# Transposing q and k of two batches by crossbar transfers in place of TensorE, in a fused attention and MLP kernel

## The chip, the cores and the metric

One core of one Trainium2 chip. The metric is device time in microseconds (us) of one execution; a median over several executions is quoted. Executions of one kernel differ by a per cent or two here. Each one carries a state, fast or slow (slow: more than 1.5% above the fastest of the same kernel). Ratios compare fast ones only; the medians in the tables are over all executions.

## The reference, cut to what matters

Four batches, eight heads, 768 rows, head size 64. Causal attention; three heads see every earlier key, five see the first 4 keys and a window of 64. The heads side by side form x of 768 x 512, which goes through a wave MLP:

```python
scores = q @ k.T / 8;  a = softmax(masked scores);  x = a @ v      # per batch and head
theta = x @ w_theta                                                # 512 x 512
zr, zi = x * cos(theta), x * sin(theta)
y = einsum('ts,bsd->btd', w_tok_r, zr) + einsum('ts,bsd->btd', w_tok_i, zi)   # the token mix, 768 x 768
u = x + y
out = u + maximum(u @ w_ch, 0)                                     # the channel matmul
```

The matmuls work on bf16. The inputs are so small (0.1 times normal draws) that the softmax is nearly uniform: an output wrong in q or k can still pass the comparison with the reference.

## The kernel before: the parts that matter

The program first writes down all steps with an engine, a duration and their dependencies. A list scheduler, steered by a long list of priorities (`TILT`), then fixes one order for each engine, and the steps are emitted in it. Each engine and each queue works through its own list in that order.

```python
def turn_qk(what, b, n):                 # 12 narrow transposes on TensorE into one PSUM bank: L395 in the profile
    pt = state["pt", what, n] = mine_bf()
    for j in range(NB):
        for x, h in enumerate(PAIRS[n]):
            nc.tensor.transpose(pt[64 * x:64 * x + 64, j * 128:(j + 1) * 128], state[what, b][:, h, j * D:(j + 1) * D], ident)

def keep_qk(what, n):                    # PSUM -> qT or kT, on VectorE or ScalarE
    dst = (qT if what == "q" else kT)[n]
    copy(dst.rearrange("d (p j) -> d p j", j=NB), state.pop(("pt", what, n))[:, :S].rearrange(...))

def load_v(b, half):                     # on the Sync queue, four heads at a time
    heads = slice(4 * half, 4 * half + 4)
    nc.sync.dma_start(out=v_room[:, heads]..., in_=v[b, heads]...)
# ...
# send_x and send_u: transposing transfers of x and u (128x512) from Sync; theta and channel matmuls wait for them
# load_qk: loads of q and k with a cast, issued from GpSimd; store: output from Sync
# mlp_steps: mix (3 groups), u, transpose of u, channel matmul, final operation, store
```

The softmax here doesn't subtract the row's maximum and nothing guards it: scores larger than these inputs give would overflow.

Of the kernel before, what the change touches and what calls it, by code (L numbers as in the profile page):

```python
# [25 lines left out]
    71383, 33577, 73294, -468, 272, 1817, 2121, 1841, 1484, 998, -351, -458, -9998906, -4244, 10993, 53854, -3405,  # L26
    6928, 42937, -27592, 3470, 440, -1170, -8668, 30584, 1187, 131611, 11003, 41350974, 22079, 7061, 59467, 66431,
    42364, 66838, 49232, 30363, 39667, 30343, 71323, 34095, 32360, 33997, 32661, 1599, -643, 481689, -687, 479643,
    10008299, 117742521, 135319420, 117742203, 135320132, 117742437, 135319441, 33665, 30756, 33818, 32757, 33944,
    32167, 96740665, 96740841, 96741207, 96740837, 96740995, -40086, 2489, -29404, 1496, 21511, 2417553, 21872,  # L30
    2417414, 1232, 23224485, 19914, 2417541, 36373805, 2417413, 41478, 20144064, 41910, 7510594, -1006, 10008162,
    27019, 10008687, 2317, -822, 71, 885, 30746, 4782, 28260, -700, 0, 851, 30200, 1234, 16671, -417, 8, -563,
    150, -315, 119, -744, 0, -2086, 0, 548, 3112, 184, 1256, -1791, 0, 218, 752, 196, 3175, -1205, 0, 71357, 6153,
    0, 32543, 49107, 31384, 1227, 34083, 31606, 41910, 2709, 478753, 42322, 1021, 20513511, 10009579, 33487,
    32376, 10009719, 3061386, 20516550, 22990, 135320173, 30384, 2419544, 52082, 68040, 33791, 31401, 59232,
    65497, 71091, 33781, 31241, 33656, 31212, 42036, 19480, 2416926, 79160287, 135318358, 36388668, 9882286,
    36359654, 9867371, 36386091, 9881900, 36360748, 9867822, 36380489, 9885853, 36359579, 16622892, 36360622,
    16626254, 36361168, 16622969, 36361066, 16623202, 4404, 16351, 59586, 28353, 4287, 16466, 36361251, 53261,
    16623326, 16375, 27903, 27573, 27919, 27740, 4295, 4300, 16459, 2029, 29794, 30117, 29643, 30164, 4475, -856,
    24, -2541, 30238, 13762, 8711, 13664, 36359955, 9868033, 53378, 28516, 4917, 16623645, 4811, 16623892, 7, 810,  # L40
    -2223, 740, 30630, 137, 686, 2190, 658, 5916, 2615, 6222, 0, 8869, 3362, -1287, 0, -358, -620, -1072, 378,
    -1088, 358, -1482, 0, -908, 3108, 3053, 2556, 3175, 1994, -541, 4029, -2027, 443, 3087, 6247, 7224, 7707,
    3524, 1446, 145, 28321, -1758, 3046, 3213, 1938, -265, 9029, 2043, 3371, 1753, 3145, 1901, 3091, 5532, 2593,
    3883, -1311, 3122, 3196, 1921, -469, 3313, 2509, -288, 569, 2781, 3713, 9243, 7431, 1470, 0, -192, 3831, 2019,
    0, 952, 2262, 2765, 1417, 4943, 2862, 3017, 627, 4671, 2631, 1041, 6646, 4670, 830, 1866, 27, 4080, 5248,
    5671, 6705, 5103, 5667, 5732, 5378, 7798, 3719, 5937, 5989, 4277, 5669, 5648, 5767, 10067, 15, 5805, 6197,
    3753, 6052, 4214, 4158, 27275, 4065, 3679, 484, 76, 699, 0, 8188, 2442, -2323, 3242, -771, 336, 0, 417, 3878,
    502, 6390, 0, 6397, 0, -201, -390, 2653, -1, 2536, 1439, 0, 27303, 4094, -1220, 699, 571, -377, 0, -2008,
    -550, 489, 1174, 4261, -521, 0, 2334, 3007, 3186, 357, 0, 539, 0, 381, 1594, 769, 681, -1176, 2403, 0, 1644,
    1424, 4167, 4774, -640, 3694, 4115, 1590, 52, 0, 10207, 10302, 17, 5487, 2487, 3322, 3685, 1958, -115, 0,  # L50
    1278, 435, 48, 4630, -7, 1570, 41, 4926, 2732, 2867, 316, -65, 3820, 5940, 46, 5714, -87, 4029, 6008, -900, 0,
    207, 3181, -1890, 0, 372, 425, 2534, 0, 2651, 0, 2938, 7089, 5815, 3035, 4150, -1419, 3038, 4396, -900, 4748,
    3928, 2180, -198, 4640, 4240, -232, 6156, 6885, 5623, 13470, 2411, 1320, 13077, 2453, 2898, 7265, 2931, 3846,
    2887, 7384, 303, 4693, 4266, 2983, 2820, 7808, 332, 2714, 7985, 7738, 3942, 2085, 7081, 13673, 1381, 1001, 97,
    13671, 1776, 2404, 0, 5385, 1277, 2572, 1913, 5381, 904, 2631, 0, 8668, 2704, -145, 1307, 12055, 2019, 142,
    1807, 2720, 2655, 1600, 11967, 4387, 5544, 4391, 5600, 4716, 3728, 2582, 1586, 1908, 1795, 1896, 2095, 3728,
    4504, 11880, 11792, 7607, 1480, 6181, -150, 2513, 3028, 3771, -520, 0, -904, 0, 1201, -1294, 774, 512, 5429,
    1558, 0, 4756, 4685, 3735, -27, 0, 1552, 0, 1212, 347, 0, 2223, 7107, 183, 0, -58, 525, 2032, 6140, 0, -349,
    0, 4456, 229, 3887, 3367, 1689, -826, 0, 13058, 12693, 2337, -246, 1411, -277, 787, 626, -2065, 0, 160, 1199,
    10944, 0, 566, 672, 136, 3705, 10380, 15055, 8015, -17, -1058, 0, 3989, 2971, 1172, 7388, -1070, 0, -401,  # L60
    1423, -2036, 0, 69, 7506, -199, -504, 1956, 8487, 284, 1558, -1901, 622, 1946, 496, 4131, -680, 1961, 7942,
    283, 1343, -1901, 2642, 0, 2935, 2901, -904, 0, 1807, 1884, 661, 0, 1498, 0, 8019, -368, -1831, 6187, 1508,
    13580, 7853, 1348, 13206, 5432, 3571, 1546, 14303, 6167, 1616, 13539, 8035, -553, 887, 6033, 3284, 1481, 8104,
    -515, 7983, -35, 5380, 3520, 4327, 2710, 14882, 4300, -225, 17476, 8037, -229, -2170, 8078, -355, -251, 5364,
    3027, 17524, 37247, 1593, 30869, 0, 37555, 1626, 31594, 0, 22131, 16141, 30282, 0, 21805, 16036, 30305, 41,
    4508, 977, 226, 1349, 2832, 1057, 18, 51, 2854, 2844, 89, 586, 8778, 8244, 8472, 4657, 2899, 2748, -123, -320,
    2283, 2087, 2174, 2098, 1672, 830, -790, -660, 5071, 4133, 3088, 3855, 7423, 7062, 9000, -975, -2753, 3331,
    5493, 1307, 31137, 0, 7964, 7870, 5312, 965, 29975, 54853, 5490, 15749, -619, 0, 587, 9022, 6186, 31738,
    30293, 285, 3736, 15797, -632, 0, 4912, 1715, -342, 1335, -509, 1610, 2359, -3159, -23, 0, 5374, 4362, 4287,
    16854, -304, 53, 2629, 2970, 285, 0, 4350, -993, 1817, 5218, -757, 1251, 2672, -1073, 1792, 0, 2872, 2629,  # L70
    2714, -1232, 767, 0, -1425, 1125, 2390, 0, 4905, 2655, -1663, -651, 2319, 3164, 28456, 141, 20332, 0, 2632,
    2284, -2379, 1034, 2273, 4363, 27747, 1034, 21235, 0, -669, 764, 12072, -454, 19612, 25792, 28797, 881, 21566,
    2456, 28301, 29807, 31171, 921, 30773, 934, 1327, 2527, 20772, 571, 28258, 1526, 1729, 1013, 679, -1128, 2221,
    2979, 21483, 744,
# [3 lines left out]
class Step:  # L78
# [7 lines left out]
    def __init__(self, on, fn, after, take, give, mode, bias, port, share):  # L86
        self.on, self.fn, self.after = on, fn, [a for a in after if a is not None]
        self.take, self.give, self.mode, self.bias, self.port, self.share = take, list(give), mode, bias, port, share
        self.eng = next(iter(on)) if len(on) == 1 else None
        self.users = 0  # L90
        self.slot = self.start = self.end = self.ns = None


class Plan:
# [18 lines left out]
    def add(self, on, ns, fn, after=(), take=None, give=(), mode=None, bias=0, port=False, share=None):  # L113
        s = Step(on if isinstance(on, dict) else {on: ns}, fn, after, take, give, mode, bias, port, share)
        for g in s.give:
            g.users += 1
        self.steps.append(s)
        return s

    def order(self, free):  # L120
# [8 lines left out]
        for s in reversed(self.steps):  # L129
            far = max(self.LATENCY[e][0] for e in s.on)  # L130
            near = min(self.LATENCY[e][1] for e in s.on)
            rank[s.n] = min(s.on.values()) + max((rank[n.n] + (near if len(s.on) == 1 and n.on.keys() == s.on.keys() else far) for n in later[s.n]), default=0)
# [24 lines left out]
        while events:  # L157
# [10 lines left out]
            for e in engines:  # L168
# [34 lines left out]
                if s.share:  # L203
                    o = "DMA" if e == "DMAH" else "DMAH"
                    rest = max(0, free.get(o, 0) - t) + sum(n.on[o] for n in ready.get(o, ()) if ready_at[n.n].get(o, 0) <= t)
                    ns += min(rest, ns * s.share) * (1 - 1 / s.share)
# [5 lines left out]
                far, near = self.LATENCY[e]  # L212
                heapq.heappush(events, (s.end, count, None))
# [19 lines left out]
def kernel(  # L233
# [40 lines left out]
    half_pi = const.tile([128, 1], F32, name="half_pi")  # L274

# [42 lines left out]
    def mine_bf():  # L318
        return mine().bitcast(BF16)
# [41 lines left out]

    def load_v(b, half):
# [627 lines left out]
```

## Time and profile before

| | before |
|---|---|
| median, three executions | 191.59 us (189.45 to 192.15) |
| span of the profiled execution | 188.3 us |
| TensorE / VectorE / ScalarE / GpSimd busy | 180.1 / 130.7 / 103.9 / 60.0 us |
| TensorE transposes of q and k (L395) | 384 matmuls, 8.0 + 7.7 us |
| queue of the Sync engine (q1) | 43256 packets, 17.65 MB, 43.5% |
| last mixing matmul to the end of the span | 181.72 to 188.3, 6.6 us |

The percentage of a queue is the time that its packets took, as a share of sixteen engines over the whole span. In a short stretch this share can exceed 1, so it is not a busy time; read it as pressure. A bank is a piece of PSUM, TensorE's output memory, and a pair is two of them; u, x, qT, vx and so on are the program's names for its tiles. PE in the profile is TensorE, DVE is VectorE, ACT is ScalarE, POOL is GpSimd, SP or SPq is the Sync engine's queue.

### The profile page before, as it was taken

Reading aid. Unit: us, or ns where it says so; the run is one execution under the profiler, and the core shown is the slowest. Engines: PE = TensorE matmul, PEld = TensorE weight load, DVE = VectorE, ACT = ScalarE, POOL = GpSimd, SP = SyncE. Lnnn points to the kernel's source line nnn. Section 1 sums busy time; section 2 is a strip of 40 time slices with the busy share of each in tenths; the row PEclk is TensorE's granted clock in tenths of the full one; section 3 lists DMA queues with packets and bytes.
Section 4 is the critical chain, followed back from the end, with each engine's and each line's share of the span. In section 5 each row is a group of like instructions: output and inputs, shape, how many; then the busy total and the mean of one; then the engine's idle time right before and its main releaser. Section 6 shows DMA issues by size and latency. Waiting matters only on the chain.

```text
span 188.3 us, 5126 instructions
## 1 busy us (share of the span) xinstructions
PE 180.1 (96%) x2143; PEld 101.2 (54%) x2143; DVE 130.7 (69%) x250; ACT 103.9 (55%) x129; POOL 60.0 (32%) x131
## 2 busy tenths in 40 slices
PE   6699989999999999999999999999999999999982
PEld 6546687764545874454447366444346564444430
DVE  7757696999855986997446466997249259935451
ACT  4488856698777707575780449686860356400010
POOL 7889878109737200005570020500320100000000
PEclk9999999999999999999999999999999999999999
DMA  5999999999999995978999952242344523234323
GB/s 175 173 188 205 200 206 204 208 207 222 147 234 274 196 136 139 209 158 187 181 128 228 104 159 41 61 95 111 87 111 58 168 59 79 61 120 106 108 111 113
DMA packets 56174, 28.06 MB, mean 149 GB/s; under 512 B 40408, under 2 KB 53080, under 8 KB 56152
## 3 DMA queue, kind: packets, MB, share of 16 engines
q1 hardware_dynamic: 43256, 17.65, 43.5%
q0 software_dynamic: 12896, 10.09, 36.1%
q8 instruction: 16, 0.26, 0.6%
q14 instruction: 6, 0.05, 0.1%
HBM read 25.71 MB, written 6.29 MB: 170 GB/s over the span
## 4 chain that ended last, share of the span: by engine, by line
PE 90%; DMA 3%; DVE 3%; ACT 2%; issue 1%; POOL 0%; POOLq 0%
PE bank L602 34%; PE bank L625 12%; PE pair L579 11%; PE pair L462 10%; PE pair L553 9%; PE bank L395 7%; DMA kb<-in_k_dram 3%; PE bank L348 2%; DVE vx L322 2%; PE bank L646 2%; PE bank L615 1%; ACT P L484 1%; PE bank L565 1%; PE pair L529 1%; ACT qT L322 0%
## 5 line engine op out<-in xcount | busy, mean ns | idle before, releaser
L602 PE MATMUL bank<-zr,wtokTr 128*128 128x512 bf16 x144 | 38.7, 380 | 0.0
L602 PE MATMUL bank<-zi,wtokTi 128*128 128x512 bf16 x144 | 38.5, 380 | 0.0
L329 POOL TENSOR_SCALAR_AFFINE_SELECT P<-P 128x256 bf16<-128x256 bf16 (+1 forms) x48 | 16.4, 359 | 45.5 <-ACT P L484 38.4
L606 DVE TENSOR_TENSOR u<-x,bank 128x512 bf16<-128x512 bf16 x24 | 16.5, 686 | 20.1 <-PE bank L602 20.1
L625 PE MATMUL bank<-w_ch_sb,uT 128*128 128x512 bf16 x96 | 24.7, 380 | 0.7 <-ACT uT L322 0.7
L462 PE MATMUL pair<-qT,kT 64*64 64x128 bf16 (+6 forms) x380 | 23.5, 238 | 0.2
L579 PE MATMUL pair<-w_theta_sb,xT 128*128 128x512 bf16 x96 | 23.5, 379 | 0.0
L484 ACT ACTIVATE P<-pair 128x1024 bf16<-128x1024 f32 (+2 forms) x24 | 21.3, 918 | 3.7 <-PE pair L462 3.6
L602 PEld LDWEIGHTS <-wtokTi 128*128 128x128 bf16 x144 | 13.3, 98 | 16.0 <-issue 0.9
L384 POOL COPY kS<-kT 64x4 bf16<-64x4 bf16 x20 | 8.8, 442 | 39.7 <-DVE kT L322 36.8
L462 PEld LDWEIGHTS <-kT 64*64 64x64 bf16 (+1 forms) x380 | 12.3, 102 | 16.2 <-issue 12.0
L602 PEld LDWEIGHTS <-wtokTr 128*128 128x128 bf16 x144 | 12.8, 98 | 15.0 <-issue 1.5
L481 ACT ACTIVATE P_st<-pair 128x1024 bf16<-128x1024 f32 (+1 forms) x16 | 12.7, 810 | 14.1 <-PE pair L462 13.9
L629 DVE SCALAR_TENSOR_TENSOR ot<-bank,u 128x512 f32<-128x512 f32 x24 | 16.4, 689 | 4.8 <-PE bank L625 4.5
L584 ACT ACTIVATE ct<-pair,half_pi 128x1024 f32<-128x1024 f32 x12 | 13.4, 1116 | 7.9 <-PE pair L579 4.6
L560 DVE TENSOR_TENSOR x<-pair,r 128x512 bf16<-128x512 f32 x24 | 16.6, 691 | 0.8
L325 DVE TENSOR_TENSOR zr<-x,ct 128x512 bf16<-128x512 bf16 x24 | 15.9, 688 | 1.7 <-ACT ct L584 1.6
L325 DVE TENSOR_TENSOR zi<-x,st 128x512 bf16<-128x512 bf16 x24 | 15.9, 688 | 0.0
L553 PE MATMUL pair<-vt,P_st 128*128 128x65 bf16 x120 | 14.9, 193 | 0.0
L553 PE MATMUL pair<-vx,P_st 128*128 128x65 bf16 x120 | 14.9, 193 | 0.0
L553 PE MATMUL pair<-vt,P 128*128 128x65 bf16 x252 | 14.1, 194 | 0.7 <-DVE x L560 0.7
L322 ACT COPY uT<-bank 128x512 bf16<-128x512 bf16 x4 | 2.3, 586 | 22.3 <-PE bank L615 22.3
(89 smaller groups left out, 289.7 us busy)
## 6 DMA issues: line engine op xcount, KB each, us to landing
out_dram<-ot SPq DMA_DIRECT2D x24, 256.0 KB, 2.8
v_room<-in_v_dram SPq DMA_DIRECT2D x6, 768.0 KB, 7.4
kb<-in_k_dram POOLq DMA_DIRECT2D x13, 192.0 KB, 5.9
qb<-in_q_dram POOLq DMA_DIRECT2D x13, 192.0 KB, 6.2
wtok<-in_moe_w_tok_r_dram POOLq DMA_DIRECT2D x3, 384.0 KB, 7.2
v_room<-in_v_dram POOLq DMA_DIRECT2D x2, 384.0 KB, 7.4
wtok<-in_moe_w_tok_i_dram POOLq DMA_DIRECT2D x2, 384.0 KB, 7.8
vx<-vt SPq DMA_DIRECT2D x3, 195.0 KB
```

What stands on the lines that cost most here:

```text
L325: {"DVE": nc.vector, "POOL": nc.gpsimd}[state["step"].eng].tensor_tensor(o, a, b, ALU.mult)
L329: nc.gpsimd.affine_select(out=t, in_=t, compare_op=ALU.is_ge, fill=fill, base=base, pattern=pattern, channel_multiplier=cm)
L462: nc.tensor.matmul(ps[half, yy, c:c + w], l, r, start=True, stop=hide is None, skip_group_check=True)
L484: nc.scalar.activation(P.rearrange("p (y c) -> p y c", y=2), ps[:, :, :w0], AF.Exp, scale=scale)
L553: nc.tensor.matmul(o, l, r, start=(m == 0), stop=True, skip_group_check=True)
L560: nc.vector.tensor_tensor(dst, av[:, :, :, :D], r.unsqueeze(3).to_broadcast([128, 2, 4, D]), ALU.mult)
L579: nc.tensor.matmul(ps[:, y], state["xT", b][:, kk, (i + y) * 128:(i + y + 1) * 128], w_theta_sb[:, kk], start=(kk == 0), stop=(kk == KD - 1))
L584: nc.scalar.activation(t, state["th", b, i], AF.Sin, bias=half_pi)
L602: nc.tensor.matmul(py, wtokT[n][:, s, t * 128:(t + 1) * 128], z[:, s], start=(g == 0 and m == 0), stop=(g == 2 and m == 3))
L606: nc.vector.tensor_tensor(u, state["x", b][:, t], state.pop(("py", b, t)), ALU.add)
L625: nc.tensor.matmul(pc, uT[:, kk], w_ch_sb[:, kk], start=(kk == 0), stop=(kk == KD - 1))
L629: nc.vector.scalar_tensor_tensor(ot, state.pop(("pc", b, t)), 0.0, state.pop(("u", b, t)), ALU.max, ALU.add)
```

## The change

Its intent: TensorE is busy 96% of the span, so take work from it. For batches 3 and 4 (indices 2 and 3) VectorE puts two heads side by side, a transposing transfer turns that tile on its way through the crossbar, and the keeping copy reads SBUF in place of PSUM. So that the loads of q and k do not fill the transfer engines at the wrong time, each waits behind a one-element read of u on GpSimd. V is loaded two heads at a time, the last block is worked off in two halves, and all priorities are new. The core:

```diff
+    def pair_qk(what, b, n):
+        h0, h1 = PAIRS[n]
+        room = mine()
+        state["qp", what, n] = t = room[:, 0].rearrange("p (j x d) -> p j x d", j=NB, x=2)
+        state["pt", what, n] = room[:, 1]
+        nc.vector.tensor_copy(t, state[what, b][:, h0:h1 + 1:2].rearrange("p x (j d) -> p j x d", d=D))
+
+    def send_qk(what, n):
+        nc.sync.dma_start_transpose(state["pt", what, n]..., state.pop(("qp", what, n))...)
 ...
-    def load_v(b, half):
-        heads = slice(4 * half, 4 * half + 4)
+    def load_v(b, n):
+        heads = slice(2 * n, 2 * n + 2)
 ...
+                if b in BY_DMA:                                   # BY_DMA = (2, 3)
+                    pair = add("DVE", 330, ...pair_qk..., [landed[what, b, n]], take="wtok", port=True)
+                    tp = add("SP", 1250, ...send_qk..., [pair])
+                    land = add("DMAH", 900, None, [tp], share=5.2, late=800)
+                    kept[what, b, n] = add({"DVE": 900, "ACT": 1500}, 0, ...keep_qk..., [land] + old, give=[pair], port=True)
+                    continue
 ...
+    def paced_load(what, b, n, heads):
+        nc.gpsimd.tensor_copy(pace, state["u", b - 2, n][:1, :1])
+        load_qk(what, b, heads)
 ...
+            if (b, t) == (B - 1, NB - 1):
+                last_steps(b, t)          # u, transposes, copies, channel matmuls, final operation and store in halves
+                continue
 ...
 TILT = [ ... 854 numbers replaced by 905 ... ]
```

## The prediction

> **What bounds the kernel now.** I read the page's first two parts, then the chain of waits, then the groups by form, then the queue of the Sync engine. The shares of the engines and the 40 slices come first.
>
> ```profile
> PE 180.1 (96%) x2143; PEld 101.2 (54%) x2143; DVE 130.7 (69%) x250; ACT 103.9 (55%) x129; POOL 60.0 (32%) x131
> ...
> PE   6699989999999999999999999999999999999982
> ...
> DVE  7757696999855986997446466997249259935451
> ...
> DMA  5999999999999995978999952242344523234323
> ```
>
> The reader is to see that TensorE is idle only in the first 25 us and the last 6. I asked for its waits between 58 and 183 us: there are none. So in that stretch, microseconds taken from TensorE's list come off the end one for one, as long as nothing else becomes late. VectorE is at 70% and the DMA row is full until about 110 us, then at 0.2 to 0.5.
>
> The chain in order of time confirms it: it runs over TensorE nearly without a break. These are its pieces for the transposes of q and k (L395) of batches 3 and 4 (indices 2 and 3), with two neighbours:
>
> ```profile
> 58.86 0.79 PE bank L395 x24
> ...
> 79.59 1.13 PE bank L395 x36
> 80.71 2.70 PE bank L602 x12
> ...
> 84.06 0.46 PE bank L395 x12
> ...
> 92.24 0.79 PE bank L395 x24
> ...
> 108.89 0.79 PE bank L395 x24
> ...
> 116.07 1.12 PE bank L395 x36
> ...
> 119.89 0.46 PE bank L395 x12
> ...
> 124.29 0.79 PE bank L395 x24
> ...
> 171.13 2.59 PE bank L602 x12
> ```
>
> Counted back, 96 transposes belong to each batch (8 tiles of 12), so these eight pieces, 192 transposes, are just those that the change removes.
>
> The groups by form give what the replacement uses, and the page's DMA part the transposing transfers that already exist:
>
> ```profile
> L322 DVE COPY qT<-bank 128x768 bf16<-128x768 bf16 x9 | 8.6, 956 | 2.2 <-PE bank L395 2.2
> L322 DVE CAST vt<-v_room 128x768 bf16<-128x768 f32 x12 | 6.2, 562 | 2.4 <-PE pair L553 2.4
> L322 ACT COPY qT<-bank 128x768 bf16<-128x768 bf16 x7 | 5.6, 803 | 4.1 <-PE bank L395 4.1
> ...
> xT<-x SPq DMA_TRANSPOSE x18, 2.4
> ```
>
> **What the Trainium skill says.** (1) "TensorEngine Tiling (Array Packing)", Key Properties: changing the tiling mode drains TensorE. The trace agrees: twelve mixing matmuls take 2.70 us after the 128x64 transposes and 2.59 us undisturbed, 0.11 us for the switch. (2) "DMA: Bandwidth & Descriptors", Issuing engines are not separate DMA queues: transfers from Sync and GpSimd run on the same 16 engines and interleave. The trace agrees as far as it can: loads of q and k of one size land in 4.3 to 9.9 us[...]. (3) "VectorE: DVE Perf Modes", What auto-detection actually checks: a copy of 16-bit data within SBUF can go four elements a cycle, a strided one at most two. With that page's 150 cycles of overhead, two a cycle gives (384 + 150) / 0.96 = 556 ns for 768 columns; the cast of V has 562. (4) "Perfetto Trace Analysis", Identifying the Most-Contended Engine: matmul busy time does not measure the distance to the roofline. True here too (weight loads are busy 54%), but the instruction order keeps TensorE without waits, so fewer instructions is what counts.
>
> **The change part by part.**
>
> *Removed from TensorE.* Batch 3: 0.79 + 1.13 + 0.46 + 0.79 = 3.17 us. Batch 4: 0.79 + 1.12 + 0.46 + 0.79 = 3.16 us. Together 6.33 us. Five of the eight pieces follow 64-row scores, so a switch stays there anyway; three stand between 128-row groups, so 3 x 0.11 = 0.33 us of switches go too. Sum 6.7 us, all of it on the chain. It also frees a PSUM bank sixteen times.
>
> *Added on VectorE.* Sixteen gathering copies (two heads side by side, bf16 in SBUF): at four a cycle, estimated from (3), (192 + 150) / 0.96 = 356 ns, so 5.7 us. The sixteen copies into qT and kT stay, but from SBUF instead of PSUM, with strided reads: between 556 ns (two a cycle, if the strided read allows it) and the 956 ns of today. In the old trace nine of these sixteen were on VectorE (8.6 us) and seven on ScalarE. The program's own plan prices ScalarE at 1500 ns for them, so most go to VectorE: 8.9 to 15.3 us in place of 8.6. VectorE in all: +6 to +12 us. In the old trace it is busy 29.2 + 24.0 + 18.6 = 71.8 us between 58 and 160 us (70%); afterwards some 78 to 84 in about 95 us, 82 to 88%. None of it is on the chain at first, but the slack is halved.
>
> *Added on the Sync queue.* Sixteen transposing transfers. A 128x512 one takes 1.20 us of the queue (median 1196 to 1217 ns) and lands 2.4 us after its start. At 128x768 I take 1.2 to 1.8 us, according to whether the issue grows with the size: 19 to 29 us. Between 64 and 140 us the queue today issues 12 transposes of x, 9 of u, about 17 stores of 0.53, 8 moves of 0.61 and 2 loads of V: 25.2 + 9.0 + 4.9 + 1.1 = 40 us of 76. Afterwards it is 60 to 70 us of about 70. This is the tightest of all the sums.
>
> *V by two heads.* Four loads instead of two for each batch, half as large: two more issues of about 0.5 us, and VectorE's casts can start sooner. The old loads landed in 7.4 us (median), and V of batch 4 is loaded at 75 and 81 us and cast at 115, so there is no wait to remove. Worth 0; its purpose is shorter blocks between the transposes on the shared engines.
>
> *The small read on GpSimd.* Eight pairs of loads get a copy of one element in front, which waits for u of two batches before. Up to now the loads started when the buffer was free: for batch 4 between 86.6 and 97.2 us, while its transposes came from 108.9 us. The read spreads them and keeps them from meeting the crossbar transposes. Cost: 16 x about 0.1 us on an engine that is 32% busy. Risk: a load that starts later lands later.
>
> *The last block in halves.* Today the last mixing matmul is followed by u 0.69 (beside a filling group of TensorE), transposes 0.33, copy 0.59, matmuls 1.04, final operation 0.69, then the store. The half copy on ScalarE is about 0.38 (the line through 590 ns at 512 and 803 at 768), so 0.21 us less; the last half of the final operation about 0.42, so 0.27 less; two halves of u cost 0.15 more; the shorter store perhaps 0.2 less. Sum about 0.5 us, all on the path.
>
> *The new order.* The whole list of priorities is replaced, the start included, where TensorE still idles about 3 us and runs 72 filling matmuls. I can't work this out from the trace and put it at 0 plus or minus 1 us.
>
> Everything taken: 6.7 + 0.5 = 7.2 us, so 191.6 - 7.2 = 184.4 us, 3.8% faster.
>
> **The rivals.**
>
> *A. The Sync queue becomes the bound.* It is served in order, so a store or a transpose of u that waits for VectorE holds the transposes of q and k behind it. For it: the sum of 60 to 70 us in 70. Against: until the change it waits much of the time (19.3 us for x, 18.0 for the output), and mixing of the batch before can fill TensorE. If it holds, TensorE shows gaps before scores or before the channel matmuls in 60 to 130 us; 3 to 6 us come back: 187 to 190 us.
>
> *B. VectorE becomes late.* For it: at 65 to 85 us it is busy 17.5 of 20 us already, and batch 3's copies fall there. Against: it waits 20.1 us in the whole run for TensorE's mixing, and the end is idle. It would cost 1 to 3 us: 185.5 to 187.5 us.
>
> *C. The 16 DMA engines are full while batch 3 is transposed.* For it: the DMA row at 9 up to slice 22. Against: at 65 to 85 us the share is 0.88, not 1.2, and batch 4 falls where it is 0.45. A late landing of one or two tiles: 1 to 2 us.
>
> *D. The gain is not on the path.* Then 191 us. Against it stands the missing wait of TensorE over 125 us; I hold it for unlikely.
>
> **Range and chances.** I expect part of A, B and C: about 1.9 us of the 7.2 given back, so **186.3 us**. If all holds and the start gains a little: 182.5. If A holds fully: 190.5. The line of 2% is 191.6 x 0.98 = 187.8 us; the change falls short of it if less than 3.8 of the 7.2 us survive. The runs of the kernel before spread from 189.45 to 192.15, which widens both sides. Chances: faster 0.62, within 2% 0.32, slower 0.06.
>
> **What would show it.** Right: L395 falls from 384 to 192 matmuls and TensorE's busy time by about 6.5 us to some 173 us; no wait of TensorE over 0.5 us between 30 and 175 us; VectorE busy 137 to 143 us; last matmul about 7 us earlier. The first step is wrong if TensorE's busy time falls but the span does not: then the chain names what it waits for, Sync's transposes for A, VectorE's copies for B, the landing of q or k for C. The size of the new copy settles the VectorE term (556 or 956 ns), and the length of the 128x768 issue the Sync term. Should the tail after the last mixing matmul not shrink by about 0.5 us, the halves did nothing. The prediction fails upward if two of the rivals meet in the stretch from 65 to 95 us, and downward if the new order also shortens the start.

## The result, and the profile after

The changed kernel took 198.63 us (median of four, 198.16 to 201.52, the last one slow); the kernel before, in the same rounds, 190.72. The ratio is **1.0405, with a 95% interval of 1.0291 to 1.0518: slower by 4%**, where 2.8% faster was predicted. Ratios here are the mean of one kernel's fast executions over the mean of the other's fast executions of the same rounds, so not quite the ratio of the medians.

First the page of the changed kernel: TensorE's line, then rows of 40 slices (tenths busy; PEclk is TensorE's granted clock in tenths).

```profile
PE 176.1 (90%) x1939; PEld 98.5 (50%) x1962; DVE 132.1 (67%) x266; ACT 109.5 (56%) x132; POOL 69.8 (36%) x147
...
PE   6699999999997909999999959799999999999981
...
PEclk9999999999999985999999999999999999999998
DMA  5999999996799997759999999864139475134513
```

A slice is 4.9 us. The PE row, unbroken before from the seventh slice on but for the end, now has holes: the 13th and 15th slices (7 and 0) and the 24th and 26th (5 and 7). In the slice after the deepest hole, which ends at 73.7 us, the granted clock is at 5 tenths. The count of weight loads (1962) tells that 23 matmul records are missing, so small gaps are not to be read.

What TensorE waited for in the changed kernel (sum in us, times, longest). Before, between 58 and 183 us, there was no such line:

```profile
PE pair L590 <- DMA xT<-x: 6.5, 3, 5.0
...
PE bank L636 <- DMA uT<-u: 2.1, 2, 1.9
...
PE pair L564 <- DMA vx<-vt: 1.2, 1, 1.2
```

All three releasers are transfers that were already there before: the transposed x and u, and the shifted V (vx). None is a transposed q or k tile. The chain of waits of the changed kernel (start, us, what) shows the new transfers as well:

```profile
51.02 9.01 DMA vx<-vt
...
64.12 5.59 DMA wtok<-wtok
...
69.79 3.84 DMA xT<-x
...
73.67 1.89 PE pair L590 x4
...
109.13 8.25 DMA wtok<-wtok
```

`wtok<-wtok` is the new crossbar transfer (it borrows the buffers of the token weights). Four theta matmuls then take 1.89 us; at full clock four take 0.86. That is the clock after a hole of about 5 us: the Trainium skill, "TensorE: Matmul & The Clock Gate", Part 1, says that TensorE falls to half its clock after an idle window of about 3.4 us and needs at least about as long under load to come back. The trace agrees on the fall: the granted clock drops to 0.50 at 72.4 us, 3.7 us after TensorE's last matmul before the hole. It is back at 1.00 at 79.3 us, after 5.6 us of work; from 75 to 80 us it is 0.57 on average.

The Sync queue around that hole (start, us, what; one row can hold several issues, the count is at its end):

```profile
53.64 5.41 SPq L364 DMA_DIRECT2D v_room<-in_v_dram  x2
59.16 6.17 SPq L410 DMA_TRANSPOSE wtok<-wtok  x2
65.43 1.05 SPq L678 DMA_DIRECT2D out_dram<-ot  x2
66.53 2.75 SPq L388 DMA_DIRECT2D vs_f<-in_v_dram  x5
69.79 5.12 SPq L579 DMA_TRANSPOSE xT<-x  x4
```

A tile of x is ready at 61.5 us but goes out at 69.79, when all that stands ahead of it in the queue has been issued. A crossbar issue that normally takes 1.21 to 1.26 us (minimum and median of the sixteen) took 4.79 us here, and a V load 3.30 (median of twelve 0.58). The issuing itself is held up.

An account of the 8.2 us between the spans (196.5 and 188.3), from tables of busy time in stretches of 5 us: L395 7.7 us less; TensorE idle between 50 and 135 us 10.6 us (before: 0); halved clock from 70 to 80 us about 2.5 us (busy time times one minus the clock); the rest, some 2.8 us, is in the start (0.9 us more of filling matmuls, 0.6 us more idle before 50 us) and after 135 us (0.9 us more idle, of which the tail is 0.5), with 0.4 us left over.

### The profile page after: what moved, and what is told of

Its sections match the earlier page's. It is cut to its first block, busy times and chain, and to the rows that moved or that the text cites. A ratio compares the mean times of both kernels' runs of the same rounds, so it can differ in the third digit from the quotient of the medians.

```text
span 196.5 us, 4826 instructions
## 1 busy us (share of the span) xinstructions
PE 176.1 (90%) x1939; PEld 98.5 (50%) x1962; DVE 132.1 (67%) x266; ACT 109.5 (56%) x132; POOL 69.8 (36%) x147
## 4 chain that ended last, share of the span: by engine, by line
PE 67%; DMA 23%; DVE 5%; issue 2%; ACT 1%; POOL 0%; SPq 0%; DVEq 0%
PE bank L613 28%; DMA wtok<-wtok 9%; PE pair L590 9%; PE pair L473 8%; PE pair L564 6%; PE bank L636 6%; DMA vx<-vt 5%; DMA xT<-x 4%; DMA qb<-in_q_dram 4%; PE bank L395 2%; PE bank L692 2%; PE bank L349 2%; DMA uT<-u 1%; DVE u L617 1%; PE bank L1026 1%
## 5 line engine op out<-in xcount | busy, mean ns | idle before, releaser
L613 PE MATMUL bank<-zr,wtokTr 128*128 128x512 bf16 x132 | 36.6, 380 | 0.8 <-issue 0.5
L384 POOL COPY kS<-kT 64x4 bf16<-64x4 bf16 x20 | 14.2, 709 | 58.2 <-ACT kT L323 33.6
L590 PE MATMUL pair<-w_theta_sb,xT 128*128 128x512 bf16 x92 | 24.9, 401 | 7.0 <-DMA xT<-x 6.5
L636 PE MATMUL bank<-w_ch_sb,uT 128*128 128x512 bf16 x88 | 22.8, 380 | 2.3 <-DMA uT<-u 2.1
L617 DVE TENSOR_TENSOR u<-x,bank 128x512 bf16<-128x512 bf16 x23 | 15.8, 685 | 10.1 <-PE bank L613 9.9
L640 DVE SCALAR_TENSOR_TENSOR ot<-bank,u 128x512 f32<-128x512 f32 x23 | 15.7, 688 | 9.9 <-PE bank L636 6.5
L613 PEld LDWEIGHTS <-wtokTi 128*128 128x128 bf16 x144 | 13.5, 98 | 15.7 <-issue 0.2
L330 POOL TENSOR_SCALAR_AFFINE_SELECT P<-P 128x256 bf16<-128x256 bf16 (+1 forms) x48 | 17.6, 390 | 6.5 <-ACT P L495 4.1
L590 PEld LDWEIGHTS <-xT 128*128 128x128 bf16 x96 | 9.3, 101 | 17.7 <-DMA xT<-x 6.0
L323 ACT COPY uT<-bank 128x512 bf16<-128x512 bf16 (+1 forms) x4 | 1.8, 480 | 25.9 <-PE bank L654 18.9
```

The costliest lines, as they stand in the source:

```text
L330: nc.gpsimd.affine_select(out=t, in_=t, compare_op=ALU.is_ge, fill=fill, base=base, pattern=pattern, channel_multiplier=cm)
L384: nc.gpsimd.tensor_copy(kS[n][rows, c:c + n_sink], kT[n][rows, :n_sink])
L590: nc.tensor.matmul(ps[:, y], state["xT", b][:, kk, (i + y) * 128:(i + y + 1) * 128], w_theta_sb[:, kk], start=(kk == 0), stop=(kk == KD - 1))
L613: nc.tensor.matmul(py, wtokT[n][:, s, t * 128:(t + 1) * 128], z[:, s], start=(g == 0 and m == 0), stop=(g == 2 and m == 3))
L617: nc.vector.tensor_tensor(u, state["x", b][:, t], state.pop(("py", b, t)), ALU.add)
L636: nc.tensor.matmul(pc, uT[:, kk], w_ch_sb[:, kk], start=(kk == 0), stop=(kk == KD - 1))
```

## The experiments

Fifteen kernels ran after the result, in four groups. Every expectation was written before its group ran. A ratio rests on two to six fast executions of the run; differences of less than about 1% are not resolved.

| run | what it is | median us | ratio to before, 95% |
|---|---|---|---|
| a_free | changed, no crossbar sends | 192.08 | 0.997 (0.984 to 1.010) |
| a_nowait | changed, sends that nobody waits for | 200.37 | 1.047 (1.038 to 1.057) |
| a_nopace | changed, without the small read | 201.06 | 1.049 (1.038 to 1.060) |
| a_spq | changed, other order in the Sync queue | 203.36 | 1.058 (1.049 to 1.066) |
| a_free_nopace | changed, no sends, no read | 189.82 | 0.995 (0.989 to 1.001) |
| b_xload | before + 16 idle sends | 201.26 | 1.044 (1.030 to 1.059) |
| b_xload4 | before + 8 idle sends, late | 191.16 | 1.005 (0.999 to 1.012) |
| b_v2 | before + V by two heads | 190.93 | 1.000 (0.991 to 1.008) |
| b_tail | before + last block in halves | 191.28 | 0.999 (0.993 to 1.006) |
| b_x4 | before + crossbar for batch 4 | 199.48 | 1.045 (1.039 to 1.050) |
| b_x4b | the same, decoupled | 201.07 | 1.055 (1.051 to 1.060) |
| b_x4c | the same, last six pairs only | 194.86 | 1.014 (1.006 to 1.022) |
| b_noturn | before, less work on TensorE, no sends | 190.61 | 1.002 (0.996 to 1.007) |
| b_noload | before, without loads of batch 4's q, k | 190.39 | 0.999 (0.991 to 1.006) |
| b_noturn_noload | both | 187.61 | 0.983 (0.978 to 0.989) |

### Is it the crossbar transfers? And which side of them: their own landing, or their load?

**a_free** drops the sends; the keeping copies read the gathered tile. Its output is wrong, which doesn't matter for the time.

```diff
-        state["pt", what, n] = room[:, 1]
+        state["pt", what, n] = room[:, 0]
-        nc.sync.dma_start_transpose(state["pt", what, n]..., state.pop(("qp", what, n))...)
+        state.pop(("qp", what, n))
```

> The changed kernel with its sixteen crossbar transfers of q and k left out: the copies into qT and kT read the gathered tile instead, so the result is wrong on purpose. Every instruction of TensorE, VectorE, ScalarE and GpSimd and its order stay; only the Sync queue loses sixteen entries. Theory Q (the transfers load the 16 DMA engines and the in-order Sync queue, and everything behind them comes late): 184 to 188 us, TensorE without waits above 1 us after 30 us. Theory L (the scores wait for the landing of their own q and k): the same, 184 to 188. Theory O (the new order, the paced loads or V in four loads cost the time, with or without the transfers): 194 us or more.

Measured 0.997. So the sends make 4.4 of the points between 0.997 and 1.0405, some 8 us. But the kernel without them is only as fast as before, although TensorE has its 192 transposes less. Its profile fell in a slow execution; which waits remain is read from a_free_nopace below.

**a_nowait** sends in full into a second tile, while the copies read the gathered one: the load is there, the wait for it is not.

```diff
-        state["pt", what, n] = room[:, 1]
+        state["pt", what, n] = room[:, 0]
+        state["into", what, n] = room[:, 1]
-        nc.sync.dma_start_transpose(state["pt", what, n]..., ...)
+        nc.sync.dma_start_transpose(state.pop(("into", what, n))..., ...)
```

> The changed kernel with its sixteen transfers sent in full and in the same place, but the copies into qT and kT read the gathered tile and wait for no transfer (wrong result on purpose). Theory Q: hardly better than the changed kernel, 194 to 198 us, with waits of TensorE for xT, uT and vx as before. Theory L: most of the loss is gone, 185 to 190 us. Theory O: no change, 197 to 200 us.

Measured 1.047, no better than with the wait. The theory that the landing of q and k alone sets the pace falls.

**a_nopace** drops the one-element read.

```diff
-        nc.gpsimd.tensor_copy(pace, state["u", b - 2, n][:1, :1])
```

> The changed kernel without the small read on GpSimd ahead of the loads of batches 3 and 4, all else and its order kept. If the read makes the loads late (they were issued at 103 to 111 us for batch 4, against 86 to 97 us in the kernel before), the loss shrinks to 191 to 195 us and the loads of batch 4 go out 5 us or more earlier. Theory Q: the loads only change places with other traffic, 196 to 201 us.

Measured 1.049; its interval overlaps that of the changed kernel. The read is not the cause.

**b_xload** is the cleanest test: the kernel before, order and all, with sixteen transposing transfers of a constant added where TensorE turns q and k of batches 3 and 4. Nobody reads them.

```diff
         # in turn_qk, after the transposes on TensorE
+        if b > 1:
+            nc.sync.dma_start_transpose(<a free weight buffer>, w_theta_sb...[:, :S])
```

> The kernel before, its order kept, with sixteen transposing transfers of 128x768 added where TensorE transposes q and k of batches 3 and 4; they read a constant and write a buffer that nobody reads (result right). It adds only the load on DMA engines and Sync queue. Theory Q: 193 to 199 us, waits of TensorE appear for xT or uT. Theory O or L: within 1% of the kernel before, 189 to 193 us.

Measured 1.044: by itself the load costs what the whole change costs. Its queue line, and the chain and Sync queue of this run:

```profile
q1 hardware_dynamic: 56056, 20.80, 53.0%
```

```profile
63.93 8.16 DMA xT<-x
100.47 8.45 DMA uT<-u
```

```profile
55.79 7.95 SPq L401 DMA_TRANSPOSE wtok<-w_theta_sb  x2
```

Sixteen transfers add 12800 packets (56174 in all before, 68974 here), 800 each. x and u, which land in 3.3 and 6.5 us at most before, now take up to 8.2 and 8.4. Two idle sends occupy the Sync queue for 7.95 us. In packet time one costs (0.530 x 196.3 - 0.435 x 188.3) / 16 = 1.38 us of all sixteen engines. This is an estimate; the eight late ones of b_xload4 (below) give 1.24 in the same way. "Load" means both things at once here, the place in the Sync queue and the time on the transfer engines: no run separates them.

**a_spq** asks whether another order in the Sync queue helps: two V loads and the sink loads (of V's first 4 rows) behind the transposes of x.

```diff
+    later = [<two V loads of batch 3, the sink loads>]
+    order = [s for s in order if s not in later]
+    order[at:at] = later                    # at: just behind the last of the first four transposes of x
+    order.remove(by[250])                   # the cast of the sinks, on VectorE
+    order.insert(order.index(by[248]) + 8, by[250])
```

> The changed kernel with three entries of the Sync queue moved: two of the loads of V for batch 3 and the five small loads of the sinks go behind the first four transposes of x of batch 2 instead of ahead of them. All else kept. If blocking in the in-order queue is the way in which the full DMA engines reach TensorE, the wait for xT at 64 to 74 us shrinks from 5 us to under 2 and the clock stays at full: 193 to 196 us. If the DMA engines themselves set the pace, the landing stays late whatever the order: 197 to 201 us.

A miss in time: 1.058, still slower. But its first theory holds for the hole that it aimed at: x goes out at 61.81 us in place of 69.79, and TensorE's waits for x fall from 6.5 to 1.3 us. A new wait came, of TensorE before the transposes of the token weights, and behind it one of VectorE:

```profile
PE bank L692 <- DVE ot L640: 7.7, 1, 7.7
```

```profile
DVE vs L1001 <- DMA vs_f<-in_v_dram: 9.7, 1, 9.7
```

That one is made by the edit: it put the cast of the sinks six operations earlier in VectorE's list than in the changed kernel, and the loads that the cast needs later. So "all else" was not kept, and what the queue's order alone is worth stays open.

### The small parts

**b_v2**, V by two heads alone on the kernel before:

```diff
-        heads = slice(4 * half, 4 * half + 4)
-        nc.sync.dma_start(...)
+        for h in (4 * half, 4 * half + 2):
+            heads = slice(h, h + 2)
+            nc.sync.dma_start(...)
```

> The kernel before with each half load of V (four heads) issued as two loads of two heads at the same place; nothing else. If the finer V loads are what jams the Sync queue in the changed kernel: 194 us or more and issues of V of several us. If they only share the engines with the rest: within 1% of the kernel before, 189 to 193 us.

1.000. Worth nothing, as predicted.

**b_tail**, the last block in halves alone on the kernel before: every operation from u to the store of the last block as two of half the columns, order kept.

> The kernel before with its last block of 128 tokens in halves (u, transposes, copy, channel matmuls, final operation and store), its order kept. By the prediction's sum 0.5 us less: the stretch from the end of the last mixing matmul to the end of the span falls from 6.6 to about 6.1 us; the time is the same within the noise (189 to 192 us). If the halves do nothing even where the halved block is the last, the stretch stays at 6.5 us or more.

0.999; half a microsecond would not show in that. The stretch from the last mixing matmul to the end shows it: 183.60 to 190.4, 6.8 us, against 6.6 before and the 6.1 expected. The chain of b_tail at its end:

```profile
185.19 1.17 PE bank L637 x8
...
186.39 0.42 DVE ot L647
```

The first half of the final operation begins only when all eight half-wide matmuls are through (at 186.36), so these two don't overlap; the matmuls cost 1.17 in place of 1.05 us. In the changed kernel the halved block isn't even the last one on TensorE:

```profile
190.58 0.87 PE bank L665 x8
191.45 0.88 PE bank L636 x4
...
192.35 0.69 DVE ot L640
```

L665 are the halves, and the whole block L636 comes behind them.

### The crossbar for batch 4 only

**b_x4** takes the kernel before and gives only batch 4's pairs to the crossbar, sent 7 us ahead of the place of the transposes. It was to be the version that keeps the gain.

```diff
+    BY_DMA = (3,)
+    ahead = sorted(((max(tp.start - 7000, land.end + 1500), fn) for tp, land, fn in pairs), ...)
     for s in order:
+        while ahead and ahead[0][0] <= s.start:
+            ahead.pop(0)[1]()               # gather on VectorE, send from Sync
```

> The kernel before with only batch 4's q and k through the crossbar, gathered and sent 7 us ahead of the place where TensorE transposed them, that is after 97 us, where the DMA row has fallen below a half; order otherwise kept. TensorE loses 96 transposes and about 3.2 us of work. Theory Q (the harm is the load on full DMA engines and the in-order Sync queue, so it is small where both have room): 187 to 190 us, 1 to 1.7% faster than the kernel before, waits of TensorE below 1 us in sum after 100 us. If crossbar transfers hurt anywhere: 192 us or more.

A miss: 1.045. The expectation had also misread the DMA row: in the kernel before the share is 1.49 from 100 to 105 us and falls to 0.55 only then, and the first send went out at 102.25. ScalarE, which works in order, stood before a keeping copy for 8 us, and TensorE then stood for ScalarE:

```profile
ACT qT L322 <- DMA wtok<-wtok: 8.0, 1, 8.0
```

```profile
PE pair L593 <- ACT st L600: 6.7, 1, 6.7
```

**b_xload4** puts eight idle sends on batch 4's places only.

```diff
-        if b > 1:                           # b_xload
+        if b > 2:
```

> The kernel before, order kept, with eight dummy crossbar transposes of a constant, only where batch 4's pairs are turned (from about 105 us on), where the transfer engines are less full than while batch 3 is turned. Theory Q1 (the sends harm only where the transfer engines are already full): 190 to 192.5 us, within 1% of before. Theory Q2 (a send blocks the Sync queue for some us wherever it is, and the transfers of x and u behind it are late): 194 to 199 us, 2 to 4% slower.

1.005: nearly free. The sends went out from 110.2 us on, none of their issues took over 1.28 us, and TensorE has no new wait above 0.4 us. So these sends did not block where the transfer engines had room (share 0.2 to 0.55 in the kernel before); the DMA row is full up to about 105 us.

**b_x4b** is b_x4 with every coupling that I could find removed: gathering into batch 3's tile, eight rooms, up to 9 us ahead, copies forced to VectorE.

> The kernel before, with batch 4's q and k alone through the crossbar, and every coupling of the earlier such run taken away: the gathering copies write into batch 3's q and k tile, the transposed tiles have eight rooms of their own, sends are up to 9 us ahead, and the keeping copies are all on VectorE, so that ScalarE waits for no transfer. It takes 3.3 us from TensorE. Theory S (the earlier run lost through the in-order wait on ScalarE alone): 187 to 190 us. Theory Q2 (the sends themselves delay the transfers of x and u): 192 us or more.

A miss: 1.055. Two things in its trace, the chain and VectorE's waits:

```profile
97.49 7.48 DMA uT<-u
```

```profile
DVE qT L403 <- DMA wtok<-qb: 5.1, 1, 5.1
```

Being "ahead" put the first send at 99.6 us, among the loads of batch 4, where a tile of u, issued at 97.49, was late already; another went out only at 113.07 us, behind others in the Sync queue, and VectorE stood 5.1 us for its landing. VectorE works in order too, so it took ScalarE's place. The coupling had moved, not gone.

### Why does less work on TensorE gain nothing even without sends?

**a_free_nopace** takes the read away from a_free too: perhaps the paced loads landed too late.

> The changed kernel with neither the sixteen crossbar sends (the keeping copies read the gathered tile, so the result is wrong on purpose) nor the small read on GpSimd; the run without the sends alone stood at 0.997 of the kernel before, although TensorE has the same 192 transposes less. Theory P (the paced loads land late and VectorE, which works in order, waits for them in its gathering copies, so that stores and x transfers go out late): 185 to 189 us, 2 to 4% faster than before. Theory O (the new order of the steps and the loads of V stand in the way by themselves): 190.5 to 193.5 us, as without the sends alone.

0.995, between the two theories and near the second: what the pacing costs is too small to see (0.997 with it). The gain of some 7 us still doesn't show. Two of the waits that remain, in a fast execution; there is one of 0.5 us for vx as well:

```profile
PE pair L590 <- DMA xT<-x: 2.1, 1, 2.1
...
PE bank L636 <- DMA uT<-u: 0.7, 1, 0.7
```

**b_noturn** asks the question in the old kernel: no crossbar, order kept, and each turned pair of batches 3 and 4 replaced by one wide matmul into the same bank. Its output is wrong, which doesn't matter for the time.

```diff
+        if b > 1:
+            nc.tensor.matmul(mine()[:, :S // 2], ident, w_theta_sb[:, 0, :S // 2], start=True, stop=True)
+            return
```

> The kernel before, order and loads kept, with each of the 16 turned pairs of batches 3 and 4 (12 narrow transposes each) replaced on TensorE by one matmul of 384 columns into the same bank (wrong on purpose); nothing goes through the crossbar. It takes about 6.7 us of transposes away and adds 16 x 0.17 = 2.7, so 4 us of TensorE's work. Step 1 of the prediction (TensorE's work comes off the end one for one): 186.5 to 188.5 us, about 2% faster. Theory N (something other than TensorE, such as transfers of x and u or VectorE, is so close behind that work taken from TensorE in the middle turns into waits): 189.5 to 192 us, same.

1.002. L395 falls from 15.7 to 8.3 us, the replacement costs 4.1, so TensorE has 3.3 us less to do, and the end doesn't move. TensorE gets this wait:

```profile
PE bank L628 <- DMA uT<-u: 2.6, 1, 2.6
```

**b_noload** and **b_noturn_noload** test what that wait says. The first drops the loads of batch 4's q and k (batch 3's are used again), with all of TensorE's work; the second drops both.

```diff
+        if b == B - 1:
+            state[what, b] = state[what, b - 1]
+            return
```

> The kernel before without the loads of batch 4's q and k (they are not loaded; batch 3's tiles are used once more, so the result is wrong on purpose); TensorE's work and the order are kept. It is the control of the next run. Theory D (in the kernel before the transfers run just ahead of TensorE, so that both bound it at once): TensorE still has all its work, so 189 to 191.5 us, same. If the transfers alone bound it: 187 us or less.

> Both taken away: the 3 to 4 us of transposes of batches 3 and 4 on TensorE (as in the run that came out at 1.002) and the loads of batch 4's q and k, which fill the transfer engines between 86 and 105 us. Theory D: with the transfers out of the way TensorE's work does come off the end, 186.5 to 188.5 us, 1 to 2% faster than before and than either taken away alone. Theory E (VectorE's and ScalarE's chain of x and u, or the order, holds the end, not the transfers): 189.5 to 191.5 us, same.

0.999 and 0.983. Take away TensorE's work: nothing. Take away the loads: nothing. Take away both: 1.7%, which is 0.017 x 190 = 3.2 us, all of the 3.3 us taken from TensorE. The stretch of 90 to 105 us shows why (busy us of each engine with instruction counts, then granted clock, DMA share, GB/s), for the kernel before, b_noturn, b_noload and b_noturn_noload:

```profile
90.00:105.00 15.00, 15.00 (x199) 8.17 (x198) 9.20 (x18) 6.90 (x10) 6.07 (x15) 1.00 1.39 166
```

```profile
90.00:105.00 15.00, 12.41 (x167) 6.74 (x166) 8.33 (x16) 5.99 (x7) 4.95 (x13) 1.00 1.34 164
```

```profile
90.00:105.00 15.00, 14.70 (x195) 8.20 (x198) 9.11 (x18) 7.05 (x10) 2.06 (x9) 1.00 0.32 64
```

```profile
90.00:105.00 15.00, 14.64 (x188) 7.85 (x190) 9.04 (x18) 6.78 (x10) 1.84 (x8) 1.00 0.31 75
```

With the loads the DMA share is 1.3 to 1.4, and the transposed u lands in up to 6.5 us (before) and 8.8 us (b_noturn). Without them the share is 0.3, and u lands in 2.6 and 4.1 us at most. In the kernel before, u arrives just when TensorE comes to it: the tile issued at 97.3 us takes 6.2 to 6.5 us to land, and TensorE takes it at 103.52. In b_noturn the same tile went out 1.5 us earlier and landed about 1 us later, at 104.57. So a faster TensorE merely arrives earlier and waits.

**b_x4c** is the real version that these runs point to: only the last six pairs of batch 4 through the crossbar, 4.5 us ahead, all sent after the loads.

```diff
-    ahead = sorted(((max(tp.start - 9000, land.end + 3000, 90000), fn) for tp, land, fn in pairs), ...)
+    ahead = sorted(((max(tp.start - 4500, land.end + 3000), fn) for tp, land, fn in pairs if tp.start > 110000), ...)
```

> The kernel before with only the last six pairs of batch 4 through the crossbar, those that TensorE turns after about 115 us, when the loads are over; sent 4.5 us ahead, copied on VectorE. It takes 6 x 0.40 = 2.4 us from TensorE. If the harm comes only from sends that meet full transfer engines: 187.5 to 190.5 us, the first real version of the idea that isn't slower. If in-order waits on the landings take it back even there: 191.5 us or more.

A miss again: 1.014, in a noisy group (six of the eleven executions of the kernel before were slow). A piece of its chain, and a wait of TensorE:

```profile
97.87 8.49 DMA uT<-u
```

```profile
PE pair L597 <- DMA xT<-x: 2.0, 1, 2.0
```

The first, which kept TensorE for 2.5 us, lies ahead of the first send (114.6 us), so it isn't the sends' doing; it is the same tight place as in b_noturn. The second is the sends' place in the Sync queue: the tile of x was ready at 116.3 us, but stood behind a transfer of u and two sends, the later of which waited for its gathering copy on VectorE, and went out at 120.17. (In the kernel before, that tile went out as soon as it was ready.) Around this gap the clock was halved, from 121.9 to 125.3 us: eight theta matmuls took 3.19 us in place of 1.73. VectorE stood only 0.2 us for the landing of a send, but worked almost without a break from 118 to 131 us. No version tried here beats the kernel before.

## Why the prediction was wrong, point by point

**"Microseconds taken from TensorE's list come off the end one for one, as long as nothing else becomes late" is the step that failed.** The work removed was sized well (6.7 us predicted; L395 fell by 7.7), and the prediction named the sign itself: TensorE's busy time fell (180.1 to 176.1 us, although the halved clock stretched it by some 2.5) and the span did not. The missing wait on TensorE only showed that nothing it needed came late. It did not show how early these things came. A transfer of u arrives with next to no margin where the loads of batch 4's q and k fill the engines. Shown for the kernel before by the four runs with and without work and loads (1.002, 0.999, 0.983 against 1). In the prediction this was rival D, "unlikely". For the changed kernel's own order it is only argued that its missing 7 us have the same cause: a_free_nopace still waits for x, u and V, but no run of it without loads was made.

**Rivals A and C, the second step that failed, had the right mechanism and far too small a size.** C allowed "a late landing of one or two tiles: 1 to 2 us", A 3 to 6 us. The load of the sends alone cost 4.4% (b_xload), over 8 us, and a_free gave about the same back. The mis-sized term was what the sends do to the transfers beside them. I had only counted queue time, and sixteen transfers also cost about 16 x 1.38 = 22 us of all sixteen engines; how the 8 us divide between the Sync queue and the engines is not shown. A looked for gaps before scores or channel matmuls; the largest, 5.0 us, was before theta matmuls, which waited for x, in the stretch from 65 to 95 us that the prediction had named. I had noted that the row of DMA was full up to slice 22, and then set it aside because one stretch had 0.88.

**The Sync term** was right at its lower end (1.26 us for an issue; 1.2 to 1.8 predicted), and the sum of 60 to 70 us in 70 was rightly called the tightest. (It counts 17 stores between 64 and 140 us; the trace has 12, so today's 40 us are about 37. Likewise one of the five pieces that it says follow 64-row scores, the one at 124.29 us, follows scores against the sinks, 128x32. Neither changes a conclusion.) What it left out is that an issue can take much longer while the engines are full: up to 4.79 us, and 5.51 in b_xload. Not every one does: the tile of u at 97.3 us in the kernel before took 1.19 us at a share of 1.5. But the old trace held the sign already: a move of V at 76.1 us took 4.67 us to issue, where the sum put 0.61. A queue that works in order hands such a delay on to everything behind it.

**VectorE:** 132.1 us busy, where 137 to 143 was predicted. The gathering copy took 0.35 to 0.38 us (estimate 0.356), the keeping copy 0.82 to 0.85 on VectorE, inside the 0.556 to 0.956 given. ScalarE did six of them, at 1.55 us each. Busy time was not what bound; standing in order before a landing was (b_x4, b_x4b).

**V by two heads,** 0: right. **The small read** took 0.25 us on average in place of 0.1 and does no harm that shows: taking it away gave no gain beside the sends, and without them 0.995 against 0.997. **The halves,** 0.5 us: wrong; the tail went from 6.6 to 6.8 us in b_tail, where the final operation waited for all eight matmuls. **The new order,** 0 plus or minus 1 us: not contradicted (0.995 for a_free_nopace and 1.002 for b_noturn, each with less work for TensorE), but not measured by itself either.

**The clock** was in no step: a hole of some 5 us cost about 2.5 us more. And a chance of 0.06 for "slower" was too low for a change that moves work onto a resource that the profile's rows already showed full.

Still open: whether any order makes the crossbar pay. b_xload4 shows that eight late sends are nearly free as load, so what would have to go is the standing of VectorE and ScalarE before their landings (b_x4, b_x4b) and the transfers of x that stand behind the sends in the Sync queue (b_x4c).

## What to carry to other kernels

An engine without waits is not a sole bound: before taking work from it, look at how late the things it needs arrive, above all transfers in stretches where the DMA row is full, or take the work away in a fake kernel and see whether the end moves. Price a transfer in time on the shared engines and not only in issue time. In queues and engines that work in order, a wait taken away at one place can come out at the next one (b_x4, then b_x4b).

## What the Trainium skill lacked or had wrong

- "Advanced Engine Details and Errata", X-Bar Transpose (TRN2): it says that transposing transfers are as fast as regular ones, with 350 to 400 GB/s expected. Here a 128x768 bf16 tile (196608 bytes) cost an estimated 1.38 us of all sixteen engines, 142 GB/s, beside other traffic, and 800 packets (b_xload); late, beside less traffic, 1.24 us or 159 GB/s (b_xload4). So the expected bandwidth was not reached. Whether regular transfers are as slow here is not shown: the same measure gives the whole Sync queue of the kernel before 215 GB/s and the GpSimd queue 148.
- "DMA: Bandwidth & Descriptors", Issuing engines are not separate DMA queues: it calls the time to initiate a transfer usually small. On Sync a transposing one took 1.2 us at best, half of its landing time of 2.4 us, and at worst 4.79 us (changed kernel) and 5.51 us (b_xload), while the transfer engines were full. I found no page that says that issuing a local transfer can be held up then.
- "VectorE: DVE Perf Modes", What auto-detection actually checks: for the strided keeping copy out of SBUF the estimate from its rule, at two elements a cycle, was 0.556 us; 0.82 was measured on VectorE. I found no page that would have given ScalarE's 1.55 us for it, against 0.80 out of PSUM.
- "TensorE: Matmul & The Clock Gate", Part 1: it says that the clock falls after an idle window of about 3.4 us. In b_x4c it fell to 0.50 at 121.9 us, when TensorE had been idle for only 1.2 us and had worked for 1.5 of the 3.4 us before. The page gives no limit for a window that is partly busy; and in the changed kernel a gap of 1.9 us (113 to 115 us) did not lower the clock.
